# A list-scheduled attention and gated-MLP kernel: TensorE prefers products whose operands and banks have been ready for a margin

## The chip, the cores and the metric

The kernel runs on one core of one Trainium2 chip. A core has five engines, each with an instruction stream of its own that runs in order: TensorE (PE, matrix products; its weight loads are listed apart as PEld), VectorE (DVE), ScalarE (ACT), GpSimd (POOL) and SyncE (SP, which here only issues DMAs). They meet through semaphores alone. Products land in PSUM, which is used here as eight banks of 128 x 512 float32. The metric is the device time of the whole program in microseconds, lower is better. A profile is one execution with a hardware trace; times in it count from the first instruction.

## The reference

Banded attention with sink tokens over 4 batches, 8 heads, 768 positions and head width 64, and after it a gated MLP over the 3072 rows that result (width 512, inner width 1536). All inputs are float64 or float32 as numpy makes them; the output is float32.

```python
keep = is_sink | in_window                    # 4 sinks, window of 128
scores = np.where(keep, scale * q @ k.T, -1e9)
a = np.exp(scores - scores.max(-1)); a = a / (a.sum(-1) + 1e-9)
x = (a @ v) laid out as [tokens, heads * 64]
gate = 1 / (1 + np.exp(-(x @ w_gate)))
out = (gate * (x @ w_val)) @ w_out
```

## The kernel before

Attention is cut into 96 units: a batch, a head and two tiles of 128 queries each (`AT`). A unit has four steps on PE. The scores `qk` (operands `qs` and `kh`, `kl`; in the first 16 units, the plain ones, `qkT`) go into a PSUM bank, twice, once for each query tile. VectorE takes masks and the row maximum from it (`top`, which writes `P` and `negm_all`), ScalarE the exponential, and one of three engines the division by `rs`. PE then turns `P` (`turn`, product of `P` with `ident`) into another bank, out of which `wt` and `sk` are made. Last, the values (`pv`, products of `wt` with `vhl` and of `sk` with `vshl`, in plain units `vraw` and `vsraw`) fill a bank that ScalarE and VectorE empty through `low` into `xr`. From two heads' `xr` come the MLP's inputs `XH` and `XL`, a high and a low part; the matrices too are held as a high and a low part, so each product of the MLP is three.

All these banks are one pool of three, tag `a`. The MLP has two banks `m` for the products with the gate and value matrices ("up products", `XH`/`XL` with `wgh`, `wgl`, `wvh`, `wvl`, 12 for each of 12 blocks `f` of the inner width and each of gate and value, issued in halves of six) and three banks `o` (a fourth is taken from `a`) for the sums over `f` ("down products", `gh`/`gl` with `woh`, `wol`). Between them stands the gate chain: `th` on ScalarE (tanh), `th` on VectorE (times the value), `gh`, then `gl`. `wol` does not stay on the core; it is written out to `wol_d` once and loaded again for each use. The token tiles are taken in the chunks `MT`: four, two, and then three tiles at a time. `XH` and `XL` hold six tiles (`RING`). The weights are decoded from their float64 words by VectorE, ScalarE and GpSimd in the first part of the run; how a decode ranks against the units is set by `DN1` to `DR2`.

No order is written by hand. Each step is an `Op` with a priority (units by number, the MLP's PE products behind all attention, its gate chain ahead of all) and a cost on each engine that may run it. `Plan.run` plays the engines against a clock of its own: at each event it gives each free engine the op of the best priority whose predecessors have ended and whose buffers are free, and the resulting list is issued as it stands. After an op ends, a successor on another engine is ready `LAT` = 180 ns later. A buffer that comes free may be taken at that instant (`slots`). Where PE would be idle in the plan during the first 130 us and has been less than 75% active in a window of 4096 / 1.2 ns, a filler is put in, a product of `ident` with itself into bank `m` (each is two instructions in the trace).

Of the kernel before, what the change touches and what calls it, by code (L numbers as in the profile page):

```python
# [38 lines left out]
DR2 = 0.3  # L39
ALT = 1  # L40
LAT = 180.0
NEXT = dict(PE=0.0, V=60.0, A=60.0, G=60.0, Q=0.0)
UPS = 2
B_vraw = 2
# [179 lines left out]
class Tile:  # L224


    def __init__(self, pool, shape, dtype, tag, bufs=None):
        self.pool, self.shape, self.dtype = pool, shape, dtype
        self.tag, self.bufs, self.slot = tag, bufs, None
        self.uses, self.left, self.got, self.held = [], 0, None, False  # L230
# [10 lines left out]
class Op:  # L241
    def __init__(self, prio, ways, dma, busy):
        self.prio, self.ways, self.dma, self.busy = prio, ways, dma, busy
        self.after, self.before, self.tiles = [], 0, []
        self.ready = 0.0


class Plan:

# [28 lines left out]
    def run(self, warm, fill_ns, fill):  # L280
        free, slots, order = {}, {}, []
        events, n = [(0.0, 0, None)], 0
        waiting = {}
        for i, o in enumerate(self.ops):
            o.seq = i
            for t in o.tiles:
                if t.bufs:
                    slots[t.tag] = list(range(t.bufs))
            for e, _, _ in o.ways:
                free.setdefault(e, 1000.0 if e == "Q" else 1400.0)  # L290
                waiting.setdefault(e, [])

        def put(o):
            for i, (e, _, _) in enumerate(o.ways):
                heapq.heappush(waiting[e], ((o.prio + i * ALT, o.seq), o))

        for o in self.ops:
            if not o.before:
                put(o)
        for e in free:  # L300
            n += 1
            heapq.heappush(events, (free[e], n, None))
        done = set()
        dma_free, window, active, cold = 0.0, 1, [0.0] * 1000, True
        HAM = 4096 / 1.2

        def busy(a, b, frac):
            while a < b:
                i = int((a + 1e-6) // HAM)
                c = min(b, (i + 1) * HAM)  # L310
                active[i] += (c - a) * frac
                a = c

        while events:
            now = events[0][0]
            while events and events[0][0] <= now:
                _, _, what = heapq.heappop(events)
                if what is None:
                    continue
                kind, o, on = what  # L320
                if kind == "ready":
                    put(o)
                    continue
                for t in o.tiles:
                    t.left -= 1
                    if not t.left and t.bufs:
                        slots[t.tag].append(t.slot)
                for x in o.after:
                    x.before -= 1
                    same = len(x.ways) == 1 and x.ways[0][0] == on  # L330
                    x.ready = max(x.ready, now + (NEXT[on] if same else LAT))
                    if not x.before:
                        n += 1
                        heapq.heappush(events, (x.ready, n, ("ready", x, None)))
            for e in free:
                if free[e] > now:
                    continue
                held = []
                while waiting[e]:
                    key, o = heapq.heappop(waiting[e])  # L340
                    if id(o) in done:
                        continue
                    need = {}
                    for t in o.tiles:
                        if not t.held:
                            need[t.tag] = need.get(t.tag, 0) + 1
                    if any(len(slots[k]) < v for k, v in need.items()):
                        held.append((key, o))
                        continue
                    first = o.ways[0][0]  # L350
                    if first != e and BACK:
                        mine = (o.prio, o.seq)
                        wait = max(free[first] - now, 0.0) + sum(
                            x.ways[0][1] for k, x in waiting[first]
                            if k < mine and id(x) not in done and x.ways[0][0] == first
                        )
                        if wait < BACK:
                            held.append((key, o))
                            continue
                    for t in o.tiles:  # L360
                        if not t.held:
                            t.held, t.slot = True, slots[t.tag].pop(0)
                    done.add(id(o))
                    ns, fn = next((ns, fn) for w, ns, fn in o.ways if w == e)
                    if e in "VAG" and now < CROWDED:
                        ns *= CROWD
                    if e == "PE":
                        while window * HAM <= now:
                            x = active[window - 1] / HAM
                            cold = x < HOT if cold else x < WARMED  # L370
                            window += 1
                        if cold:
                            ns *= 2
                        busy(now, now + ns, o.busy)
                    order.append((o, e, fn))
                    free[e] = now + ns
                    n += 1
                    heapq.heappush(events, (now + ns, n, None))
                    n += 1
                    end = now + ns  # L380
                    if o.dma:
                        dma_free = max(dma_free, end + 650) + o.dma
                        end = dma_free + 750
                    heapq.heappush(events, (end, n, ("end", o, e)))
                    break
                for x in held:
                    heapq.heappush(waiting[e], x)
                w = int(now // HAM)
                if (
                    e == "PE" and free[e] <= now < warm  # L390
                    and active[w] < FLOOR * (now - w * HAM + fill_ns)
                ):
                    order.append((None, e, fill))
                    ns = fill_ns * (2 if cold else 1)
                    busy(now, now + ns, 1.0)
                    free[e] = now + ns
                    n += 1
                    heapq.heappush(events, (free[e], n, None))
        assert sum(o is not None for o, _, _ in order) == len(self.ops)
        self.time = now  # L400
        for o, e, fn in order:
            fn()
# [3 lines left out]
def kernel(  # L406
# [265 lines left out]
    def attend(u, b, h, t0, T, XR):  # L672
# [234 lines left out]
        if h % 2:  # L907

            c, g = h // 2, b * NT + t0
            runs = [[0]]  # L910
            for t in range(1, T):
                if chunk_of[g + t] == chunk_of[g + t - 1]:
                    runs[-1].append(t)
                else:
                    runs.append([t])
            for run in runs:
                cols = slice(run[0] * 128, run[-1] * 128 + 128)
                ts = slice((g + run[0]) % RING * 128, (g + run[0]) % RING * 128 + len(run) * 128)
                parts = [(c, (g + t) % RING) for t in run]
                x = lambda cols=cols: xr()[:, cols]  # L920
                hi, lo = lambda ts=ts: XH()[:, c, ts], lambda ts=ts: XL()[:, c, ts]
                copy(u, len(run) * 128, hi, x, [xr], [(XH, p) for p in parts], plain)
                rest(
                    u, len(run) * 128, lo, x, hi, [xr] + [(XH, p) for p in parts],
                    [(XL, p) for p in parts], plain,
                )
# [263 lines left out]
```

## Time and profile before

| | us |
|---|---|
| median of the timed runs (3: 848.28 to 850.38) | 848.75 |
| the profiled execution | 850.93 |
| its span, first to last instruction | 849.1 |
| TensorE busy | 820.3 |
| VectorE busy | 518.4 |
| ScalarE busy | 427.7 |
| GpSimd busy | 442.2 |
| bytes read from HBM, over the span | 84.77 MB |

Matmuls are pipelined and their ends in the trace are modelled: a row lasts longer than the distance to the next row's start. PE's busy time is therefore no measure of PE at its peak, and its idle time between rows is a little less than what a wait costs. Nearly every instruction is recorded through one helper, so rows are told apart by the tiles they write and read, not by line (L459 for all of them).

### The profile page before, as it was taken

Reading aid. Unit: us, or ns where it says so; the run is one execution under the profiler, and the core shown is the slowest. Engines: PE = TensorE matmul, PEld = TensorE weight load, DVE = VectorE, ACT = ScalarE, POOL = GpSimd, SP = SyncE. Lnnn points to the kernel's source line nnn. Section 1 sums busy time; section 2 is a strip of 40 time slices with the busy share of each in tenths; the row PEclk is TensorE's granted clock in tenths of the full one; section 3 lists DMA queues with packets and bytes.
Section 4 is the critical chain, followed back from the end, with each engine's and each line's share of the span. In section 5 each row is a group of like instructions: output and inputs, shape, how many; then the busy total and the mean of one; then the engine's idle time right before and its main releaser. Section 6 shows DMA issues by size and latency. Waiting matters only on the chain. (4 is left out here: it accounts for less than half of the span.)

```text
span 849.1 us, 15442 instructions
## 1 busy us (share of the span) xinstructions
PE 820.3 (97%) x4774; PEld 728.2 (86%) x4774; DVE 518.4 (61%) x1574; ACT 427.7 (50%) x1228; POOL 442.2 (52%) x615
## 2 busy tenths in 40 slices
PE   8999989899999999999999999999999999999996
PEld 6667788788888888999899988899899989999995
DVE  5767778998898999715941498935941385111110
ACT  4666778787667778605720377534720273001001
POOL 3666768786577777514741377634741272111111
PEclk9999999999999999999999999999999999999999
DMA  4567767764655454412531153432631131112111
GB/s 130 161 174 203 201 173 222 207 204 135 191 137 131 116 137 106 128 50 61 157 92 38 47 136 104 117 91 59 155 93 49 41 100 38 38 38 86 38 50 53
DMA packets 99255, 95.29 MB, mean 112 GB/s; under 512 B 44384, under 2 KB 79200, under 8 KB 99168
## 3 DMA queue, kind: packets, MB, share of 16 engines
q1 hardware_dynamic: 99168, 94.25, 40.6%
q8 instruction: 40, 0.66, 0.3%
q14 instruction: 47, 0.39, 0.1%
HBM read 84.77 MB, written 9.44 MB: 111 GB/s over the span
## 5 line engine op out<-in xcount | busy, mean ns | idle before, releaser
L459 DVE SCALAR_TENSOR_TENSOR th<-th,m 128x384 f32<-128x384 f32 (+1 forms) x108 | 54.8, 508 | 235.8 <-PE m L459 235.0
L459 POOL TENSOR_TENSOR gl<-th,gh 128x384 fp32r<-128x384 f32 (+1 forms) x62 | 61.9, 998 | 230.6 <-DVE gh L459 220.0
L459 ACT ACTIVATE th<-m 128x384 f32<-128x384 f32 (+1 forms) x108 | 49.0, 454 | 261.4 <-PE m L459 260.5
L459 POOL TENSOR_SCALAR_AFFINE_SELECT wt<-wt 128x512 fp32r<-128x512 f32 (+3 forms) x192 | 115.9, 605 | 50.9 <-DVE wt L459 33.9
L459 PE MATMUL m<-XH,wvh 128*128 128x384 f32 (+1 forms) x432 | 138.9, 322 | 0.0
L459 PE MATMUL m<-XH,wgh 128*128 128x384 f32 (+1 forms) x432 | 138.7, 321 | 0.0
L459 PE MATMUL m<-XL,wvh 128*128 128x384 f32 (+1 forms) x432 | 137.7, 319 | 0.0
L459 PE MATMUL m<-XH,wvl 128*128 128x384 f32 (+1 forms) x432 | 137.3, 318 | 0.0
L459 PE MATMUL m<-XL,wgh 128*128 128x384 f32 (+1 forms) x432 | 137.3, 318 | 0.0
L459 PE MATMUL m<-XH,wgl 128*128 128x384 f32 (+1 forms) x432 | 137.3, 318 | 0.0
L459 PE MATMUL o<-wol,gh 128*128 128x512 f32 x276 | 108.1, 392 | 4.4 <-DMA wol<-wol_d 4.4
L459 PE MATMUL o<-woh,gl 128*128 128x512 f32 x276 | 109.0, 395 | 2.2 <-DVE gl L459 1.7
L459 PE MATMUL o<-woh,gh 128*128 128x512 f32 x276 | 109.5, 397 | 1.4 <-DVE total L1144 1.0
L459 ACT ACTIVATE P<-P,negm_all 128x144 f32<-128x144 f32 x192 | 78.6, 410 | 16.1 <-DVE negm_all L459 13.5
L459 PEld LDWEIGHTS m<-XH,wvh 128*128 128x128 f32 x432 | 81.5, 189 | 4.5 <-issue 1.4
L459 PEld LDWEIGHTS m<-XH,wgh 128*128 128x128 f32 x432 | 81.6, 189 | 2.9 <-issue 1.5
L459 PEld LDWEIGHTS m<-XL,wvh 128*128 128x128 f32 x432 | 81.5, 189 | 2.8
L459 PEld LDWEIGHTS m<-XL,wgh 128*128 128x128 f32 x432 | 81.7, 189 | 0.5
L459 PEld LDWEIGHTS m<-XH,wgl 128*128 128x128 f32 x432 | 81.6, 189 | 0.0
L459 PEld LDWEIGHTS m<-XH,wvl 128*128 128x128 f32 x432 | 81.4, 188 | 0.0
L459 PEld LDWEIGHTS o<-woh,gl 128*128 128x128 f32 x276 | 51.7, 187 | 16.0 <-DVE gl L459 2.9
L459 POOL TENSOR_TENSOR qs<-qkT,qs 64x256 fp32r<-64x256 f32 x71 | 54.4, 766 | 19.6 <-issue 4.8
(118 smaller groups left out, 1737.9 us busy)
## 6 DMA issues: line engine op xcount, KB each, us to landing
wol<-wol_d SPq DMA_DIRECT2D x108, 256.0 KB, 2.9
qkT<-in_k_dram SPq DMA_DIRECT2D x120, 108.0 KB, 2.7
qkT<-in_q_dram SPq DMA_DIRECT2D x176, 64.0 KB, 2.6
wst<-in_moe_w_gate_dram SPq DMA_DIRECT2D x12, 512.0 KB, 4.5
wst<-in_moe_w_val_dram SPq DMA_DIRECT2D x12, 512.0 KB, 4.9
wst<-in_moe_w_out_dram SPq DMA_DIRECT2D x12, 512.0 KB, 4.1
vraw<-in_v_dram SPq DMA_DIRECT2D x64, 96.0 KB, 2.4
out_dram<-w SPq DMA_DIRECT2D x23, 256.0 KB, 2.9
```

What stands on the lines that cost most here:

```text
L459: return lambda *a, **kw: tc.keep_in_program_order(op(*a, **kw))
```

## The change

Three constants come in, and both rules by which `Plan.run` picks an op change. The first concerns all engines: a buffer that has come free may be taken `FREE` = 150 ns later, not at once. To that end a free slot is kept with the time at which it came free. The second concerns PE alone: each op carries a time `sure`, the end of its last predecessor on another engine plus `LAT` and `SURE` = 600 ns, or `SURE_D` = 1200 ns where that predecessor is a DMA. PE's candidates are gone through by priority as before; one that is not yet sure, or that would take a buffer which came free less than `LAT + SURE` ago, is put aside. Only when no candidate is sure, the first of those put aside is taken.

```diff
+SURE = 600.0
+SURE_D = 1200.0
+FREE = 150.0
...
-                    slots[t.tag] = list(range(t.bufs))
+                    slots[t.tag] = [(x, -1.0e9) for x in range(t.bufs)]
...
-                        slots[t.tag].append(t.slot)
+                        slots[t.tag].append((t.slot, now))
+                        if FREE:
+                            n += 1
+                            heapq.heappush(events, (now + FREE, n, None))
...
+                    if on != "PE":
+                        x.sure = max(x.sure, now + LAT + (SURE_D if o.dma else SURE))
...
-                while waiting[e]:
-                    key, o = heapq.heappop(waiting[e])
+                unsure = [] if e == "PE" else None
+                while waiting[e] or unsure:
+                    if waiting[e]:
+                        key, o = heapq.heappop(waiting[e])
+                    else:
+                        (key, o), unsure = unsure[0], unsure[1:]
+                        held += unsure
+                        unsure = None
...
-                    if any(len(slots[k]) < v for k, v in need.items()):
+                    if any(
+                        len(slots[k]) < v or slots[k][v - 1][1] + FREE > now
+                        for k, v in need.items()
+                    ):
                         held.append((key, o))
+                        continue
+                    if unsure is not None and (
+                        o.sure > now
+                        or any(slots[k][v - 1][1] + LAT + SURE > now for k, v in need.items())
+                    ):
+                        unsure.append((key, o))
                         continue
...
-                            t.held, t.slot = True, slots[t.tag].pop(0)
+                            t.held, t.slot = True, slots[t.tag].pop(0)[0]
...
-                for x in held:
+                for x in held + (unsure or []):
```

The computation and the set of products are the same; what moves is the order on every engine, and which of the permitted engines runs a step. Three places show it, all on PE. Numbers behind the names are buffers and differ between the kernels.

The first place is in the second batch of units, where an attention unit's `pv` ends (`sk_87,vshl_86`) and PE goes on to the turn of another unit (`ident,P`) and to scores (`kh`, `kl`). Before:

```order
L459 MATMUL a_3382<-sk_87,vshl_86 128x256
L459 MATMUL o_3054<-woh_120,gh_3364 128x512
L459 MATMUL o_3054<-wol_3161,gh_3364 128x512
L459 MATMUL o_3054<-woh_120,gl_3373 128x512
L459 MATMUL a_3403<-ident,P_3277 128x128
L459 MATMUL a_3403<-ident,P_3277 16x128
L459 MATMUL a_3403<-ident,P_3277 128x128
L459 MATMUL a_3403<-ident,P_3277 16x128
L459 MATMUL a_3412<-kh_3282,qs_3280 128x272
L459 MATMUL a_3412<-kl_3307,qs_3280 128x272
```

The same place now; between the two groups of up products nine more of the same kind are left out:

```order
L484 MATMUL a_3419<-sk_87,vshl_86 128x256
L484 MATMUL a_3431<-ident,P_3284 128x128
L484 MATMUL a_3431<-ident,P_3284 16x128
L484 MATMUL a_3431<-ident,P_3284 128x128
L484 MATMUL a_3431<-ident,P_3284 16x128
L484 MATMUL m_97<-XH,wgh_126 128x256
L484 MATMUL m_97<-XL,wgh_126 128x256
...
L484 MATMUL m_97<-XH,wgl_127 128x256
L484 MATMUL a_3471<-kh_3305,qs_3286 128x272
L484 MATMUL a_3471<-kl_3320,qs_3286 128x272
```

Three down products have gone from between `pv` and the scores, and twelve up products have come in behind the turn.

The second place is the last stretch with fillers, where the plain units end and too few weights are decoded for up products. Before:

```order
L459 MATMUL a_1162<-kl_1012,qs_990 128x272
L459 MATMUL a_1170<-wt_1124,vraw_1082 64x256
L459 MATMUL a_1170<-wt_1124,vraw_1082 64x128 x2
L459 MATMUL a_1170<-low_1148,vsraw 64x256
L459 MATMUL m_97<-ident 128x128 x2
L459 MATMUL a_1193<-ident,P_1103 128x128
L459 MATMUL a_1193<-ident,P_1103 16x128
L459 MATMUL a_1193<-ident,P_1103 128x128
L459 MATMUL a_1193<-ident,P_1103 16x128
L459 MATMUL a_1202<-kh_1063,qs_1070 128x272
```

The same stretch now:

```order
L484 MATMUL a_1171<-kl_1062,qs_1022 128x272
L484 MATMUL m_97<-ident 128x128 x6
L484 MATMUL a_1195<-wt_1150,vraw_1104 64x256
L484 MATMUL a_1195<-wt_1150,vraw_1104 64x128 x2
L484 MATMUL a_1195<-low_1156,vsraw 64x256
L484 MATMUL m_97<-ident 128x128 x3
L484 MATMUL a_1225<-ident,P_1118 128x128
L484 MATMUL a_1225<-ident,P_1118 16x128
L484 MATMUL a_1225<-ident,P_1118 128x128
L484 MATMUL a_1225<-ident,P_1118 16x128
L484 MATMUL m_97<-ident 128x128
L484 MATMUL a_1236<-kh_1102,qs_1097 128x272
```

Where two fillers (`m_97<-ident`) stood there are ten. In the whole program there are 70 before and 85 now, all of them in this stretch and ahead of it.

The third place is the end of PE's work, the last up products and the down products of the last block `f` (`woh_160`) and the one before it (`woh_155`). Before:

```order
L459 MATMUL o_9859<-woh_155,gl_10264 128x512
L459 MATMUL m_98<-XH,wvh_158 128x384
L459 MATMUL m_98<-XL,wvh_158 128x384
L459 MATMUL m_98<-XH,wvl_159 128x384
L459 MATMUL m_98<-XH,wvh_158 128x384
L459 MATMUL m_98<-XL,wvh_158 128x384
L459 MATMUL m_98<-XH,wvl_159 128x384
L1140 MATMUL count<-bad,one 1x4
L459 MATMUL o_9851<-woh_160,gh_10290 128x512
L459 MATMUL o_9851<-wol_10241,gh_10290 128x512
L459 MATMUL o_9851<-woh_160,gl_10292 128x512
```

The same place now:

```order
L484 MATMUL m_98<-XH,wvl_159 128x384
L484 MATMUL o_9872<-woh_155,gh_10271 128x512
L484 MATMUL o_9872<-wol_10231,gh_10271 128x512
L484 MATMUL o_9872<-woh_155,gl_10279 128x512
L484 MATMUL o_9877<-woh_155,gh_10271 128x512
L484 MATMUL o_9877<-wol_10231,gh_10271 128x512
L484 MATMUL o_9877<-woh_155,gl_10279 128x512
L484 MATMUL o_9883<-woh_155,gh_10271 128x512
L484 MATMUL o_9883<-wol_10231,gh_10271 128x512
L484 MATMUL o_9883<-woh_155,gl_10279 128x512
L484 MATMUL o_9872<-woh_160,gh_10302 128x512
```

The nine down products of the block before the last have moved behind the last up product, and `count`, a product of a check that follows the plan, has moved behind all down products.

More of the change, by code (lines that the diff above doesn't have):

```diff
@@ L244, in __init__ @@
         self.after, self.before, self.tiles = [], 0, []
-        self.ready = 0.0
+        self.ready = self.sure = 0.0
 class Plan:
```

## The prediction

> **What bounds the kernel now.** I read the page first (span, busy time), then busy time by stage, then what TensorE (PE) waited for, then single places in order of time.
>
> ```profile
> span 849.1 us, 15442 instructions
> PE 820.3 (97%) x4774; PEld 728.2 (86%) x4774; DVE 518.4 (61%) x1574; ACT 427.7 (50%) x1228; POOL 442.2 (52%) x615
> ```
>
> ```profile
> core 0: us, PE busy (x) PEld busy (x) DVE busy (x) ACT busy (x) POOL busy (x), PEclk, DMA share, GB/s
> 100.00:220.00 120.00, 109.39 (x750) 98.54 (x749) 101.78 (x246) 91.82 (x220) 91.71 (x106) 0.99 0.66 189
> 220.00:340.00 120.00, 115.78 (x763) 103.20 (x763) 110.08 (x365) 90.39 (x297) 89.15 (x137) 1.00 0.51 133
> 340.00:720.00 380.00, 375.95 (x2111) 345.20 (x2110) 221.20 (x697) 171.85 (x525) 183.23 (x266) 1.00 0.32 86
> 720.00:840.00 120.00, 119.37 (x633) 111.95 (x631) 18.03 (x41) 11.11 (x22) 19.31 (x19) 1.00 0.18 49
> ```
>
> PE is the bound: from 100 us on nothing else is near full for long, and PE's work is the same whatever its order. What an order can win is the time in which PE stands. From 720 us only the dense part runs and PE stands 0.6 us. Between 100 and 720 us it stands 10.61 + 4.22 + 4.05 = 18.9 us. DVE is the one rival engine: 110.08 of 120 us, 92%, from 220 to 340 us.
>
> PE's waits between 100 and 720 us, the five largest groups (us in total, times, longest):
>
> ```profile
> PE o L459 <- DMA wol<-wol_d: 4.4, 4, 2.2
> PE a L459 <- DVE sk L459: 4.0, 7, 1.2
> PE a L459 <- DVE xr L459: 2.6, 7, 1.0
> PE o L459 <- DVE gl L459: 1.7, 2, 1.2
> PE a L459 <- DVE negm_all L459: 1.6, 3, 1.1
> ```
>
> Most are attention products into a PSUM bank `a` that DVE has just let go. One of them in order of time:
>
> ```profile
> 246.49 0.40 PE L459 MATMUL o<-wol,gh 128*128 128x512 f32 x1
> ...
> 246.73 0.39 PE L459 MATMUL o<-woh,gl 128*128 128x512 f32 x1
> 247.06 0.42 DVE L459 TENSOR_TENSOR xr<-a,low 64x256 f32<-64x256 f32 x1
> ...
> 247.63 0.36 PE L459 MATMUL a<-kh,qs 128*128 128x272 f32 x1 [0.51 <-DVE xr L459]
> ```
>
> The scores `kh,qs` take the bank that `xr` empties; the plan of before lets PE come as soon as its own clock says the bank is free, and on the chip PE comes early. The row says 0.51 us idle. But a down product streams in 0.24 us (246.49 to 246.73) while its row, whose end is modelled, lasts 0.39; the scores could have started at 246.97 and lost 0.66 us, so each stop hides 0.15 us. The 23 stops above hide 3.5 us: PE loses 18.9 + 3.5, **about 22.5 us**, between 100 and 720 us.
>
> **Term 1, stops.** Nothing is added to the products: in the order, repeats counted, PE has 5067 rows for 5052, and all 15 more are fillers. In the changed plan a product counts as sure 600 ns after its operands and banks are there, on top of the 180 ns of `LAT` (1200 where a DMA brings them), and goes ahead of unsure ones. So a stop disappears where the plan's clock errs by less than 0.78 us (1.38 for a DMA) and another product is at hand. By the longest of each group, about 1.0 us stays of the longest `wol` stop (2.2 + 0.15 - 1.38) and 0.4 to 0.6 us of the longest in each DVE group, with the next longest some 4 us in all if the places stayed: 18.5 of 22.5 would go. The first order piece above shows it: where scores stood four transposes and three down products behind the product that feeds `low`, there are now four transposes and twelve up products. Up products are nearly always at hand: counted in the order, 696 of them (690 before) stand ahead of the end of the 33rd PV group, and the token tiles finished by then allow 864. But the new places can err too, so I take a little less, 73%, **-16.5 us**; ends: -22.5 (all) and -4 (each new place errs as the old).
>
> **Term 2, clock.** The longest `wol` stop costs twice:
>
> ```profile
> 114.06 0.40 PE L459 MATMUL o<-woh,gh 128*128 128x512 f32 x1
> 116.69 0.50 PE L459 MATMUL o<-wol,gh 128*128 128x512 f32 x1 [2.23 <-DMA wol<-wol_d]
> 117.10:120.50 3.40, 3.40 (x14) 3.01 (x13) 1.38 (x6) 0.00 (x0) 2.26 (x4) 0.50 0.78 230
> ```
>
> After 2.23 us of standing the granted clock is 0.50 for 3.4 us, half of which, 1.7 us, is lost. A stop shortened by up to 1.38 us should not do it. I take **-1.2 us** (ends -1.7, and 0 if the stop stays; +1.7 if a new one as long arises). The Trainium skill ("TensorE: Matmul & The Clock Gate", Part 1: The HAM clock gate) says that PE falls to half rate after at least one idle window of about 3.4 us. By that rule 2.6 us between two starts would be too short, and the term 0; the row shows the clock halved after it, so the row decides.
>
> **Term 3, the end.**
>
> ```profile
> 838.73 0.33 PE L459 MATMUL m<-XL,wvh 128*128 128x384 f32 x1
> ...
> 838.91 0.34 PE L459 MATMUL m<-XH,wvl 128*128 128x384 f32 x1
> ...
> 839.18 0.19 PE L1140 MATMUL count<-bad,one 128*1 128x4 f32 x2
> 839.35 0.55 DVE L459 SCALAR_TENSOR_TENSOR th<-th,m 128x384 f32<-128x384 f32 x1 [5.30 <-PE m L459]
> 839.94 0.36 DVE L459 CAST gh<-th 128x384 fp32r<-128x384 f32 x1
> 840.22 0.14 DVE L1144 TENSOR_REDUCE total<-flag 1x1 int32<-1x4 int32 x1
> 840.36 0.50 PE L459 MATMUL o<-woh,gh 128*128 128x512 f32 x1 [0.99 <-DVE total L1144]
> 840.47 1.00 POOL L459 TENSOR_TENSOR gl<-th,gh 128x384 fp32r<-128x384 f32 x1 [5.23 <-DVE total L1144]
> 840.69 0.40 PE L459 MATMUL o<-wol,gh 128*128 128x512 f32 x1
> ...
> 841.52 0.50 PE L459 MATMUL o<-woh,gl 128*128 128x512 f32 x1 [0.43 <-POOLq L1147]
> ...
> 843.02 0.40 PE L459 MATMUL o<-woh,gl 128*128 128x512 f32 x1
> ...
> 844.62 0.57 SPq L459 DMA_DIRECT2D out_dram<-qkT  x1
> ```
>
> The last gate chain (th, gh, gl) has nothing beside it: PE stands 1.45 - 0.18 = 1.27 us before 840.36 and 0.83 - 0.24 = 0.59 us before 841.52 (0.18, from 838.73 to 838.91, and the 0.24 above are what such products take in a stream). In the new order (third piece) the nine down products of the step before stand behind the last up product: 9 x 0.24 = 2.16 us, and two more until `gl` is needed, 2.64 us. `gl` was there 841.47 - 839.09 = 2.4 us after the last up product. Both stops go: **-1.9 us** (ends -1.9 and -1.3). `count` moves behind the last product: it, `flag` and `total` take 839.18 to 840.36, 1.2 us, beside ScalarE's eviction and the last output's issue at 844.62, 1.6 us after the last product's start; it costs nothing, at worst 0.5 us.
>
> **Term 4, the start.**
>
> ```profile
> L459 PE MATMUL m<-ident 128*128 128x128 f32 x140 | 26.0, 332 | 1.8 <-POOL ident masks.py:199 1.8
> 94.50:102.00 7.50, 7.03 (x49) 5.56 (x49) 4.59 (x16) 5.28 (x15) 5.05 (x9) 1.00 0.65 150
> ```
>
> A filler is two of these, so 70 become 85 (second piece). They occupy 26.0 / 70 = 0.37 us each, 15 are 5.6 us. Between 94.5 and 102 us PE fills and hardly stands (0.5 us), so fillers there lie on PE's path unless the data come no earlier. Ends: +5.6 (all on the path) and -2 (attention comes earlier, since the last weight load is row 195 of SP's DMAs instead of 204). I take **+3.0 us**, about half.
>
> **Sum.** -16.5 - 1.2 - 1.9 + 3.0 = -16.6 us. The profiled run took 850.93 us, 849.1 of span and 1.8 around it; it lies 2.2 above the median of the timed runs, so I apply the sum to that: 848.75 - 16.6 = **832 us**. The Trainium skill ("Trainium Kernel Development and Optimization", Performance Expectations) holds the weight loads' busy share to be a better gauge than the matmuls'. It is 546.94 / 620 = 88% between 100 and 720 us against 93% after, so 31 us would be open instead of 22.5, and with 73% of that the result would be 826; part of that difference is narrow products, so I keep the stops.
>
> **Rivals.** *The margin only moves the stops* (0.20): a third goes, 8 us, since DVE delivers the bank at its own pace; -8 - 1.9 + 3 = 842 us. For it: DVE's 92%. Against: PE is mostly only 0.4 to 0.6 us too early (4.0 / 7, 2.6 / 7, 1.6 / 3), and the new order gives DVE more time per attention unit: ahead of the end of the 49th PV group stand 972 up and 246 down products, against 930 and 234.
>
> *DVE sets the pace* (0.07, the other side): the order gives DVE 1732 rows for 1696, at 518.4 / 1574 = 0.33 us each 12 us more, 41% of it (211.86 / 518.4) between 100 and 340 us: 5 us. If DVE is full there (it decides from some 98% between 220 and 340 us), PE's stops there stay and grow by 5; with the whole start, 5.6, and the gain of the end and a little after 340 us, 848.75 + 5 + 5.6 - 1.9 - 2.5 = 855 us. Against it: 8% of DVE is idle there, and POOL and ACT give up the work that DVE takes.
>
> *The change does not do what it says* (0.06): PE mostly takes unsure products, for want of others; only the end gains, the start loses: 848 to 850 us. Against it: the three pieces.
>
> **Numbers.** 0.67 for the forecast (826 to 838), 0.20 for 842, 0.07 for 855, 0.06 for no change. The low bound is 22.5 + 1.7 + 1.9 with nothing lost at the start, 822.6, so 822; the high one takes in the 842 case with the whole start and one new clock dip (+2.6, +1.7), 846. Outside are the last two cases and edges, under 2 in 10. A change of 0.3% (2.5 us) is about what a measurement here can tell from none: faster 0.86, same 0.07, slower 0.07.
>
> **What would show it.** Right: between 100 and 720 us PE idle falls from 18.9 to about 6 us, `kh,qs` most; no slice at a lower clock after 100 us; no stop at the end longer than 0.2 us; fillers x170, and the last one ends near 104 us instead of 101.5. Wrong: stops of 0.5 us before `kh,qs` as before; DVE over 98% from 220 to 340 us; a last filler after 108 us; a new stop over 2 us with half the clock behind it.

## The result and the profile after

| | before | after |
|---|---|---|
| median of the timed runs, side by side (4 and 4) | 848.51 us | 828.33 us |
| ratio, 95% interval | | 0.9765 [0.9732, 0.9799] |
| the profiled execution | 850.93 us | 830.16 us |
| its span | 849.1 us | 828.5 us |

The kernel is 20.2 us faster by the medians and 20.8 by the profiled executions; forecast were 16.6 (832 us). The page of the changed kernel, span and busy times:

```profile
span 828.5 us, 15445 instructions
PE 808.2 (98%) x4804; PEld 729.3 (88%) x4804; DVE 527.2 (64%) x1610; ACT 417.9 (50%) x1197; POOL 450.6 (54%) x610
```

PE's busy time fell by 12 us though 30 fillers' rows came in: the row ahead of a stop and the row behind it last longer than in a stream, and there are fewer of both (counted below). The busy time by stage of the changed kernel (from, to, length, then PE, PEld, DVE, ACT, POOL with their rows, the granted clock, the DMA share, GB/s):

```profile
100.00:220.00 120.00, 113.24 (x796) 102.89 (x797) 103.73 (x266) 93.58 (x230) 97.57 (x112) 1.00 0.67 196
220.00:340.00 120.00, 119.29 (x790) 110.14 (x789) 110.92 (x364) 84.33 (x276) 86.51 (x129) 1.00 0.48 125
340.00:720.00 380.00, 377.94 (x2144) 351.37 (x2143) 231.03 (x719) 164.47 (x500) 192.45 (x272) 1.00 0.32 86
```

PE stands 6.76 + 0.71 + 2.06 = 9.5 us, against 18.9. DVE has 110.92 of 120 us in the second stage, 92% as before. PE's largest waits between 100 and 720 us in the changed kernel (total, times, longest):

```profile
PE a L484 <- DVE XL L484: 3.1, 1, 3.1
PE a L484 <- DVE xr L484: 1.8, 3, 0.8
PE a L484 <- DVE negm_all L484: 0.7, 2, 0.5
PE a L484 <- POOL P L484: 0.7, 2, 0.5
...
PE o L484 <- DMA wol<-wol_d: 0.5, 1, 0.5
```

A third of what is left is one new stop of 3.1 us, for `XL` at 105 us; it belongs to the start (below). Without it PE stands 6.4 us. `sk`, 4.0 us before, is down to 0.3, and `wol` from 4.4 to 0.5.

To place the rest, the run is cut at two marks that both kernels have, first the end of the 17th PV group. Before:

```profile
105.56 0.28 PE L459 MATMUL a<-sk,vshl 128*128 128x256 f32 x1
```

After:

```profile
108.87 0.28 PE L484 MATMUL a<-sk,vshl 128*128 128x256 f32 x1
```

The order puts the same 132 up products ahead of this mark in both. The second mark is the last up product, 838.91 before and 817.01 now. The end of the changed kernel in order of time:

```profile
817.01 0.34 PE L484 MATMUL m<-XH,wvl 128*128 128x384 f32 x1
...
817.18 0.39 PE L484 MATMUL o<-woh,gh 128*128 128x512 f32 x1
...
819.70 0.44 PE L484 MATMUL o<-woh,gl 128*128 128x512 f32 x1
...
821.13 0.39 PE L484 MATMUL o<-woh,gl 128*128 128x512 f32 x1
...
821.45 0.19 PE L1165 MATMUL count<-bad,one 128*1 128x4 f32 x2
821.55 0.60 ACT L484 ACTIVATE qkT<-o 128x512 f32<-128x512 f32 x1
821.67 0.15 DVE L1167 CAST flag<-count 1x4 int32<-1x4 f32 x1 [3.27 <-PE count L1165]
821.86 0.14 DVE L1169 TENSOR_REDUCE total<-flag 1x1 int32<-1x4 int32 x1
```

| stretch | before | after | difference | forecast |
|---|---|---|---|---|
| start to the 17th PV group | 105.6 | 108.9 | +3.3 | +3.0 |
| to the last up product, nine down products' 2.0 us apart | 733.3 - 2.0 | 708.1 | -23.2 | -16.5 - 1.2 |
| to the last down product, with the nine | 4.1 + 2.0 | 4.1 | -2.0 | -1.9 |
| to the end of the span | 6.1 | 7.3 | +1.3 | 0 |
| span | 849.1 | 828.5 | -20.6 | -16.6 |

What the 23.2 us are made of, counted over every row of PE between the two marks. A stop is a product that begins over 0.03 us after the end of the row before; "hidden" is what the row ahead of the stop lasts beyond its length in a stream, the distance at which rows of its shape follow each other:

| between the marks | before | after | difference |
|---|---|---|---|
| stops | 47 | 18 | -29 |
| idle in them | 18.6 us | 6.4 us | -12.2 |
| hidden in them | 7.9 us | 3.4 us | -4.5 |
| the product behind a stop slower | 3.8 us | 1.5 us | -2.3 |
| other products slower than in a stream, the clock among them | 28.5 us | 24.3 us | -4.2 |

The last line's size depends on the length taken for a stream, its difference hardly does. The fourth line was not in the prediction. Behind the stop that it showed at 247.63, the kernel before goes on with `kl,qs`; its weight loads (PEld) and this product:

```profile
247.59 0.19 PEld L459 LDWEIGHTS a<-kh,qs 128*128 128x128 f32 x1 [0.91 <-ACT wt L459]
247.70 0.19 PEld L459 LDWEIGHTS a<-kl,qs 128*128 128x128 f32 x1
247.83 0.29 PE L459 MATMUL a<-kl,qs 128*128 128x272 f32 x1
```

`kl,qs` comes 0.20 us after `kh,qs`, and its weight load began 0.07 us after `kh,qs` did (in the changed kernel it begins with `kh,qs`, at 241.39). The changed kernel at the place of the first order piece (the 33rd PV group), TensorE alone:

```profile
239.41 0.28 PE L484 MATMUL a<-sk,vshl 128*128 128x256 f32 x1
239.53 0.60 PE L484 MATMUL a<-ident,P 128*128 128x128 f32 x4
...
241.27 0.28 PE L484 MATMUL m<-XH,wgl 128*128 128x256 f32 x1
241.39 0.29 PE L484 MATMUL a<-kh,qs 128*128 128x272 f32 x1
241.52 0.29 PE L484 MATMUL a<-kl,qs 128*128 128x272 f32 x1
```

Here `kh,qs` follows twelve up products without a bracket, so without a stop, and `kl,qs` comes 0.13 us behind it. The weight load that a stop leaves uncovered costs about 0.08 us, 3.8 us over the 47 stops. So a stop costs (7.9 + 3.8) / 47 = 0.25 us beside its idle time, not the 0.15 that the prediction put.

### The profile page after: what moved, and what is told of

It reads as the page before. It is cut to its first block, busy times and chain, and to the rows that moved or that the text cites. A ratio compares the mean times of both kernels' runs of the same rounds, so it can differ in the third digit from the quotient of the medians.

```text
span 828.5 us, 15445 instructions
## 1 busy us (share of the span) xinstructions
PE 808.2 (98%) x4804; PEld 729.3 (88%) x4804; DVE 527.2 (64%) x1610; ACT 417.9 (50%) x1197; POOL 450.6 (54%) x610
## 4 chain that ended last, share of the span: by engine, by line
PE 67%; DVE 9%; ACT 3%; DMA 2%; POOL 2%; issue 2%; SPq 1%; DVEq 0%; ACTq 0%; POOLq 0%
PE m L484 38%; PE o L484 18%; PE a L484 10%; DVE sk L484 1%; DVE w L484 1%; DMA vraw<-in_v_dram 1%; SPq L484 1%; ACT P L484 1%; DVE vhl L484 1%; DVE wt L484 1%; DVE P L484 1%; DVE xr L484 1%; DVE a L484 1%; DMA qkT<-in_k_dram 1%; POOL P L484 1%
## 5 line engine op out<-in xcount | busy, mean ns | idle before, releaser
L484 POOL TENSOR_TENSOR gl<-th,gh 128x384 fp32r<-128x384 f32 (+1 forms) x73 | 70.8, 971 | 206.8 <-DVE gh L484 196.9
L484 DVE CUSTOM_DVE_ANT_0 P<-a,am 128x144 f32<-128x144 f32 x192 | 58.6, 306 | 9.6 <-PE a L484 3.2
```

Of the source, the lines that this page charges most:

```text
L484: return lambda *a, **kw: tc.keep_in_program_order(op(*a, **kw))
```

## The experiments

Each edit is made to the changed kernel. Each ratio is against the kernel before on the same chip.

**The parts: which of the three rules does it?** First the 150 ns alone, without any margin (a `sure` in the past is always sure):

```diff
-SURE = 600.0
-SURE_D = 1200.0
+SURE = -1000.0
+SURE_D = -1000.0
```

> Only the 150 ns before a freed buffer is taken again stays (all engines); PE picks by priority alone, without a margin. Margin theory (PE's stops go because sure products go first): most stops stay, PE idle between 100 and 720 us at least 14 us (18.9 before, 9.5 with the whole change), the two last stops of PE stay, time 838 to 848 us. Rival (the plan had wrongly taken freed buffers at once, and a truer plan is the gain): PE idle under 11 us and 826 to 834 us. It also tells whether the later start comes with this rule: fillers are 100 in its order.

Measured: 850.35 us, ratio 1.0022 [0.9998, 1.0045], 47 stops: no gain, even a little over the 848 us that were expected at most. The stops are shorter than before (12.5 us idle between the marks), but 100 fillers stand in this list instead of 70 and take 6 us more. Then the margins without the 150 ns:

```diff
-FREE = 150.0
+FREE = 0.0
```

> Only PE's margin stays (600 and 1200 ns); freed buffers are taken at once on all engines. Margin theory: PE idle between 100 and 720 us 5 to 10 us, time 825 to 832 us, within 0.5% of the whole change. Rival (the truer plan is the gain): 838 to 848 us.

Measured: 836.0 us, 0.9831 [0.9801, 0.9861], 30 stops. That is most of the gain, but 0.66 points less than the whole change, where at most 0.5 was expected. Next the margin for banks alone; operands count as sure at once:

```diff
-                    if on != "PE":
-                        x.sure = max(x.sure, now + LAT + (SURE_D if o.dma else SURE))
```

> The whole change, but the margin holds only for banks and buffers that have just come free, not for operands. Theory (the stops before scores, where PE wants a bank that VectorE has just emptied, are the larger part: 8.2 of the 14.3 us in the five groups of before): time 831 to 838 us, the groups behind sk, xr and negm_all together under 4 us of idle. Rival (operands are what matters; banks come free in time anyway): 840 us or more.

Measured: 838.73 us, 0.9899 [0.9856, 0.9943], 26 stops; the time lies just over the 838 us expected. And the margin for operands alone:

```diff
-                    if unsure is not None and (
-                        o.sure > now
-                        or any(slots[k][v - 1][1] + LAT + SURE > now for k, v in need.items())
-                    ):
+                    if unsure is not None and o.sure > now:
```

> The whole change, but the margin holds only for operands, not for banks and buffers. Theory: the stops behind sk, xr and negm_all stay, at least 5 us of idle, those behind wol, gl and gh go; the end gains as in the whole change; time 836 to 845 us, slower than with banks alone. Rival (operands): 826 to 832 us.

Measured: 842.64 us, 0.9950 [0.9928, 0.9972], 42 stops. The three largest groups of PE's waits in this last kernel, between 100 and 720 us:

```profile
PE a L481 <- DVE sk L481: 4.2, 7, 1.5
PE a L481 <- DVE negm_all L481: 3.1, 5, 1.1
PE a L481 <- DVE xr L481: 2.6, 6, 0.8
```

All three are banks that DVE has just let go, as large as before the change or larger (4.0, 1.6, 2.6 then). The 150 ns give nothing by themselves; the margin on banks takes away the larger part of the stops, that on operands the smaller, and each alone gives less than both. Each of these is one list, and the two controls below show how much lists of the same idea differ (0.8 and 1.4 points), so the shares of the parts, and what the 150 ns add to the margins, are rough.

**The start: are the 15 more fillers on the path?** The groups of the changed kernel have the predicted fillers, two rows each:

```profile
L484 PE MATMUL m<-ident 128*128 128x128 f32 x170 | 29.2, 316 | 1.8 <-POOL ident masks.py:199 1.8
```

In order of time at their end, SP's issues with DVE and PE:

```profile
96.09 0.53 SPq L484 DMA_DIRECT2D wst<-in_moe_w_gate_dram  x1
...
96.72 0.46 SPq L484 DMA_DIRECT2D vraw<-in_v_dram  x1
...
101.21 0.83 PE L484 MATMUL m<-ident 128*128 128x128 f32 x6
102.88 0.35 DVE L484 CAST vhl<-vraw 128x192 fp32r<-128x192 f32 x1 [4.08 <-DMA vraw<-in_v_dram]
...
104.69 0.41 DVE L484 TENSOR_TENSOR XL<-a,XH 128x256 fp32r<-128x256 f32 x1
105.15 0.19 PEld L484 LDWEIGHTS a<-kh,qs 128*128 128x128 f32 x1 [3.30 <-DVE XL L484]
105.15 0.39 PE L484 MATMUL a<-kh,qs 128*128 128x272 f32 x1 [3.11 <-DVE XL L484]
```

The fillers end at 102, and then PE stands for `XL`, which queues on DVE behind a cast that waits 4.08 us for `vraw`. That load was issued 0.6 us behind one of 512 KB and took some 6.1 us. In this profile the 15 loads of `vraw` and `qkT` issued directly behind such a load, within 1 us, took 3.0 to 6.1 us, 4.2 in the median; the other 433 took 2.5 in the median. To see what the fillers themselves cost, 20 of them are left out:

```diff
-WARM = 130000.0
+WARM = 70000.0
```

> The whole change, with no filler after 70 us of the plan's clock: 65 fillers instead of 85, none in the last stretch, everything else by the same rules. Fillers on PE's path (my term 4): PE reaches the scores behind the last stretch some 3 us earlier than the 105.15 us of the changed kernel, time 3 us lower, about 825 us. Rival (the start waits for VectorE, which stood 4.08 us for the load of vraw, and fillers only fill that wait): the same scores at 105 us within 1 us, time within 1.5 us of the whole change; should PE's clock fall for want of fillers, up to 3 us more.

Measured: 838.23 us, 0.9881 [0.9821, 0.9941]. The mark of the 17th PV group came later, at 111.0 us, not earlier. This kernel's busy time from 95 us on, for the stretch that the clock view showed at a lower clock:

```profile
95.10:108.70 13.60, 9.47 (x36) 7.07 (x37) 8.21 (x26) 7.49 (x17) 8.32 (x12) 0.50 0.80 222
```

And in order of time:

```profile
104.56 1.09 PE L484 MATMUL a<-ident,P 128*128 128x128 f32 x4 [3.60 <-DVE XL L484]
```

The wait for `XL` is still there, and without the fillers the clock is at half for 13.6 us. `vhl`'s cast began 2.4 us sooner than in the changed kernel (100.51 against 102.88), and the wait for `XL` ended 0.6 us sooner, so this run does not show that the fillers cost nothing: it changes the clock along with them. What it shows is that leaving them out does not pay, and the trace of the changed kernel shows that PE stood 3.11 us after the last one. Most of the 10 us that this kernel lost, more than either expectation allowed, lies behind the mark: 715.3 us from there to the last up product, against 708.1.

**The end: what does `count` behind the last product cost?** In the whole change the check sum (`bad`, `count`, `flag`, `total`) is issued in the order 20 entries behind the last step that uses a bank `a`, instead of behind the plan (the check itself, now a function `check`, is left out here):

```diff
...
-        for o, e, fn in order:
+        last = max(
+            i for i, (o, _, _) in enumerate(order)
+            if o and any(getattr(x, "tag", None) == "a" for x in o.tiles)
+        )
+        for i, (_, _, fn) in enumerate(order):
             fn()
+            if i == last + 20:
+                check()
...
```

> The whole change, with the check of the sizes (the product count, flag and total) issued behind the last attention product instead of behind the last product of all; the order of the plan is the same. In the changed kernel PE's branch on total began 1.8 us after the last product and took 4.5 us, and the end waited 2.5 us for it. Theory (count's move costs the end 2.5 us): the time from the last product's start to the end of the span falls from 7.3 to about 4.8 us, the time by 1.3 to 2.5 us to 826 to 827 us. Rival (the end waits for the last output's landing or the branch takes as long wherever it stands, since it follows the last product): the end stays within 0.5 us of 7.3.

Measured: 828.2 us, 0.9737 [0.9705, 0.9769]; from the last product's start to the end of the span 6.39 us instead of 7.33, where 4.8 was expected. The intervals of this ratio and of the change's own overlap, so the timed runs alone don't show the gain; the tails of the profiles do. What the tail waits for is a branch on `total` in PE's sequencer. The branch's row in the changed kernel (count: shortest/median/longest ns, first and last start):

```profile
L1172 PEldq COMPARE_BRANCH  x1: 4498/4498/4498, 822.9 to 822.9; - x1
```

SP's closing semaphore instructions in the same kernel:

```profile
L1210 SPq EVENT_SEMAPHORE  x10: 17/28/2560, 824.6 to 828.4; - x10
```

And the branch in the kernel before:

```profile
L1147 PEldq COMPARE_BRANCH  x1: 3497/3497/3497, 842.1 to 842.1; - x1
```

Before, it ran from 842.1 to 845.6, beside the last products and ScalarE's and SP's closing work. Now it begins at 822.9, 1.8 us after the last product's start, takes 4.5 us, and SP's wait of 2.56 us ends at 827.55, 0.15 us after it. In the kernel with fewer fillers, where `count` stands as late, the branch took 3.8 us and the tail 6.6. With the check sum early the branch begins 0.9 us ahead of the last product.

**The size of the margin, and luck.** Half and double:

```diff
-SURE = 600.0
-SURE_D = 1200.0
+SURE = 300.0
+SURE_D = 600.0
```

> The whole change with margins of 300 and 600 ns. Theory (a margin takes away the stops that are shorter than itself plus 180 ns; the DVE groups' stops were 0.4 to 0.6 us in the mean): about half of the gain from stops, 833 to 840 us. Rival (any preference for what is not just ready does it, its size matters little): 826 to 831 us.

Measured: 843.13 us, 0.9957 [0.9937, 0.9977], 38 stops: less than a fifth of the change's gain, where about half was expected.

```diff
-SURE = 600.0
-SURE_D = 1200.0
+SURE = 1200.0
+SURE_D = 2400.0
```

> The whole change with margins of 1200 and 2400 ns. Theory: the stops that are left after 105 us (6.4 us of idle) halve, attention comes a little later against the MLP, time 824 to 830 us. Rival (a longer margin starves attention: banks stand empty, VectorE gets its work too late, PE takes unsure products): 832 us or more, with more stops.

Measured: 824.22 us, 0.9733 [0.9682, 0.9785], 11 stops; its interval overlaps the change's. Double, with the check sum early as above:

> The whole change with the margins doubled (1200 and 2400 instead of 600 and 1200) and the check sum issued 20 entries ahead of the end. Theory (each half stands for itself): the doubled margin gave 0.9733 and the early check took the time from the start of the last down product to the end of the span from 7.33 to 6.39 us, so together ratio about 0.972, some 823 us, idle of TensorE between 100 and 720 us about 6 us, the last stretch under 6.6 us. Rival (the gains overlap, or each plan is a draw): ratio of 0.976 or more, as the change alone.

Measured: 824.52 us, 0.9743 [0.972, 0.9767], 9 stops. (The check sum stands where it stood in the run above, behind the last step with a bank `a`.) The tail went from 7.3 to 6.3 us here too, but the times show no gain over the doubled margin alone: by its ratio the rival's 0.976 lies in the interval, so this run doesn't settle it. Four times the margin (`SURE` 2400, `SURE_D` 4800), check sum early:

> As the run before with four times the margin (2400 and 4800). Theory: with 1200 and 2400 only 5.8 us of idle were left between 100 and 720 us, so at most 3 us more are to be had: ratio 0.968 to 0.976, idle 3 to 6 us. Rival (too wide a margin leaves ready attention products lying behind up products, so that the attention ends late and products of the second half lack cover): ratio above 0.978, idle after 340 us over 5 us.

Measured: 837.9 us, 0.9912 [0.9888, 0.9936]: the rival's time. But not in its place. The busy time by stage of this kernel:

```profile
100.00:220.00 120.00, 113.06 (x805) 104.16 (x804) 104.08 (x245) 90.34 (x217) 95.73 (x114) 1.00 0.66 193
220.00:340.00 120.00, 115.58 (x735) 106.74 (x735) 103.33 (x328) 71.19 (x224) 76.28 (x112) 0.96 0.41 110
340.00:720.00 380.00, 379.74 (x2180) 355.04 (x2180) 262.14 (x798) 173.26 (x524) 205.22 (x297) 1.00 0.34 91
...
285.60:295.80 10.20, 8.02 (x31) 6.73 (x30) 9.30 (x31) 6.84 (x23) 6.88 (x10) 0.50 0.46 125
```

The idle time lies before 340 us (6.9 and 4.4 us), not behind; the last row shows 10.2 us at half the clock. With the wide margin 1044 up products stand ahead of the 49th PV group instead of 972, and attention, with DVE at 86% instead of 92%, came late (the 49th PV group at 348 us instead of 323).

Last, two controls with nearly the change's own margin, 550 and 1100, then 650 and 1300:

> The whole change with margins of 550 and 1100 instead of 600 and 1200: the same idea in another plan. Theory (the margin's size decides, a plan's details little): 826 to 832 us, ratio 0.973 to 0.981. Rival (each plan is a draw, and the gain of one setting is mostly luck): anywhere from 0.97 to 0.996, the time going with the stops and the clock dips that this plan happens to have.

> The whole change with margins of 650 and 1300 instead of 600 and 1200. Theory (the margin's size decides, a plan's details little): 825 to 831 us, ratio 0.972 to 0.980. Rival (each plan is a draw): anywhere from 0.97 to 0.996, the time going with the stops and the clock dips that this plan happens to have.

Measured: 837.43 us, 0.9905 [0.9874, 0.9937], 34 stops; and 833.29 us, 0.9842 [0.9813, 0.9871], 24 stops. Theory's bounds (0.981 and 0.980) are missed by both: a margin that is 8% smaller or larger makes another list and loses 1.4 or 0.8 points of the 2.35. All runs by their stops (stops between the marks, as counted above; a lower clock from 90 us to the last up product):

| kernel | margin, ns | ratio | stops | idle in them, us | lower clock |
|---|---|---|---|---|---|
| before | none | 1 | 47 | 18.6 | 3.4 us |
| 150 ns only | none | 1.0022 | 47 | 12.5 | 3.4 us |
| operands only | 600 | 0.9950 | 42 | 17.3 | 2 x 3.4 us |
| half | 300 | 0.9957 | 38 | 11.5 | - |
| control | 550 | 0.9905 | 34 | 9.7 | - |
| without the 150 ns | 600 | 0.9831 | 30 | 11.0 | - |
| fewer fillers | 600 | 0.9881 | 27 | 11.9 | 13.6 and 3.4 us |
| banks only | 600 | 0.9899 | 26 | 10.4 | 3.4 us |
| control | 650 | 0.9842 | 24 | 7.8 | 3.4 us |
| the change | 600 | 0.9765 | 18 | 6.4 | - |
| four times, check early | 2400 | 0.9912 | 18 | 10.9 | 10.2 us |
| check early | 600 | 0.9737 | 16 | 6.2 | 3.4 us |
| double | 1200 | 0.9733 | 11 | 5.7 | - |
| double, check early | 1200 | 0.9743 | 9 | 5.7 | - |

With few stops the time is short. The three that stand out of line (banks only, fewer fillers, four times) have half the clock for a while, or kept the stops of the end (banks only and four times, 1.4 and 1.5 us idle there). Every list with a margin is faster than the kernel before; the one without is not. But the number of stops does not follow the margin step by step: 38, 34, 18, 24, 11, 18 for 300, 550, 600, 650, 1200, 2400. The direction is the margin's; its two neighbours gain 8 and 13 us (0.95% and 1.58% of 848), and what the change has beyond them is what this one list happens to avoid. No version here is shown to beat the change: the three at 0.9733 to 0.9743 lie within its interval.

## Why the prediction was right, point by point

**Term 1, the stops (-16.5): the mechanism was right, the size of what was there too small.** Idle and hidden time between the marks fell by 12.2 + 4.5 = 16.7 us. But that is 16.7 of 26.5, 63%, where 73% of 22.5 was forecast: the five groups named 23 stops, the rows hold 47. That 16.7 is so near to 16.5 is luck: too small a sum met too large a share. And the product behind each stop, another 2.3 us, had been left out, as had the part of the table's last line (4.2 us) that is not the clock's 1.7. Idle between 100 and 720 us came to 9.5 us, 6.4 without the start's stop, where about 6 was forecast. The parts show the cause: with the bank margin alone and the operand margin alone there are 26 and 42 stops, with neither 47.

**The weight loads' gauge.** PEld's busy share between 100 and 720 us went from 88% to (102.89 + 110.14 + 351.37) / 620 = 91%. The Trainium skill ("Trainium Kernel Development and Optimization", Performance Expectations) takes this share as a better gauge than the matmuls' busy time, and 826 us followed from it; 828.3 was measured, nearer to that than to 832. But of the 31 us that it held open only 564.4 - 546.9 = 17.5 closed, 56% and not 73%, so the nearness proves little. What the gauge saw and the idle rows did not is, in part, the slower product behind each stop.

**Term 2, the clock (-1.2).** No slice of the changed kernel from 100 us to the last product has a lower clock: the 1.7 us are gone, since the long `wol` stop is (0.5 us now). But the expectation that no lower clock would be left, since a shortened stop should not do it, was lucky. The new stop of 3.11 us passed at full clock. What decides can be worked out from the times at which the granted clock changes: in each of the 13 profiles that have more than one such change they lie whole multiples of 3.413 us apart, as on a fixed grid (in the changed kernel 8.23, 15.06 and 824.02 us: 2 and 237 steps). This stop, from 102.04 to 105.15, is divided by a mark of the grid, and PE is busy for 1.65 and 2.07 us of the stretches on both sides:

```profile
100.39:103.80 3.41, 1.65 (x13) 1.35 (x12) 0.92 (x3) 1.00 (x3) 0.48 (x1) 1.00 0.52 143
103.80:107.22 3.42, 2.07 (x17) 2.07 (x18) 3.25 (x13) 2.30 (x6) 3.17 (x5) 1.00 0.53 123
```

The same list with the check sum early stood less at this place,

```profile
104.52 0.60 PE L490 MATMUL a<-kh,qs 128*128 128x272 f32 x1 [2.35 <-DVE XL L490]
```

but nearly all of this stop lies in one stretch, with PE busy for 1.18 us, and half the clock follows:

```profile
100.99:104.40 3.41, 1.18 (x11) 0.99 (x8) 2.15 (x6) 0.95 (x4) 1.54 (x3) 1.00 0.49 126
...
104.40:107.80 3.40, 3.28 (x15) 3.28 (x16) 2.01 (x10) 2.50 (x7) 3.25 (x5) 0.50 0.81 227
```

So the length of a stop does not settle it; where it falls on the grid does. Between 16 us and the last products, PE's rows covered 20 to 58% of each full-clock stretch that half the clock followed, and at least 48% of each that it did not, over all 14 profiles. The Trainium skill ("TensorE: Matmul & The Clock Gate", Part 1: The HAM clock gate) says that the window of about 3.4 us runs freely and is not reset when a kernel starts; that fits the grid, and one list taking both ways. Its condition, at least one idle window, does not fit: the stretch ahead of 104.40 was 35% busy.

**Term 3, the end (-1.9): the stops went, the sentence on `count` failed.** Both stops vanished and gave 2.0 us. "It costs nothing, at worst 0.5 us" named the work that hides `count`, `flag` and `total`, and these indeed took 0.55 us (821.45 to 822.0); it forgot what reads `total`: a load and a branch in every engine, on PE 4.5 us, which the last products had covered before. 1.3 us of tail came of it, and the run with the check sum early took 0.94 of them back. Together the end gained 0.7 us of the 1.9 forecast.

**Term 4, the start (+3.0): the size was right by luck, the reason wrong.** +3.3 us were measured, but the last filler ended at 102.0 us, not near 104, and 20 fillers fewer made the start longer. The step that failed is that the 15 fillers take 5.6 us and "lie on PE's path unless the data come no earlier", of which half was taken: they took 29.2 - 26.0 = 3.2 us of busy time, the data came later, and PE stood 3.11 us after the last filler. In the fillers' place stood DVE, 4.08 us at `vraw`, with `XL` queued behind it; how far the fillers had delayed the steps ahead of that is not shown. "Attention comes earlier, since the last weight load is row 195 of SP's DMAs" looked at the last load's rank and not at what is issued just ahead of `vraw`. That the load was late for the 512 KB in front of it fits the 4.2 against 2.5 us above; no run moved that load, so its share in the 6.1 us stays open.

**The rivals.** DVE kept 92% and did not become the bound, so 855 us fell. "The margin only moves the stops" fell for this list, 47 to 18; for its neighbour at 550 it is nearly what happened (34 stops, 837 us). A third rival was missing: that the gain of one setting is partly the draw of one list, with 828 to 837 us for the same idea. The range held it (822 to 846).

## What to carry to other kernels

Where a list is planned offline and issued as it stands, a margin on resources that another engine has just released can take away most of the stops, but judge it at two or three neighbouring settings before putting the size of its gain down to the rule. Price a stop with what hides in the row ahead and with the slower product behind it (here 0.25 us beside the idle row). When a scalar result moves to the end, follow it to the branches that read it, and when a queue is reordered, look at the loads issued ahead of the one that waits.

## What the runs showed of the hardware that was not expected

A branch on a loaded value held PE's sequencer 3.5 to 4.5 us (3497, 3602 and 4498 ns in three profiles, 3462 to 4518 over all 14) where other engines' took 45 to 72 ns:

```profile
L1181 PEldq COMPARE_BRANCH  x1: 3602/3602/3602, 813.0 to 813.0; - x1
```

This row is of the kernel with double margin and early check sum, where it lies beside the last products. There `total` was ready at 706 us, over 100 us earlier, so the branch did not spend this time waiting for the value; on what it spends it is not shown. And half the clock came behind single stops of 1.76 us (operands only),

```profile
162.44 0.51 PE L481 MATMUL o<-woh,gl 128*128 128x512 f32 x1 [1.76 <-POOL gl L481]
```

by that kernel's busy time

```profile
163.30:166.70 3.40, 3.40 (x14) 2.55 (x12) 2.58 (x5) 2.33 (x3) 3.40 (x4) 0.51 0.45 143
```

while 3.11 us passed without it: the shorter stop lay whole in one stretch of the grid (159.92 to 163.33), the longer in two.
